# One tile for two heads' queries, keys and values, or two

## The chip, the cores and the metric

The kernel runs on one core of a Trainium2 chip. The metric is the device time of one execution in microseconds. The core's engines are TensorE (PE, matmuls; PEld is its weight load), VectorE (DVE), ScalarE (ACT), GpSimd (POOL) and SyncE (SP), whose queue issues every DMA of this kernel.

## What is computed

Attention with a band, then two MLP blocks, for 2 batches of 768 positions, 8 heads of 64 and a model width of 512. Cut to what matters:

```python
keep = is_global | is_local               # the first 8 keys, and the last 96
scores = scale * (q @ k.T) - slopes * dist
scores = where(keep, scores, -1e9)
a = exp(scores - max) ; a = a / (sum(a) + 1e-9)
x = a @ v                                 # (B, H, S, D), brought to (B, S, H*D)
# block 1: over positions, then over channels
h = maximum(x.T @ w_tok1, 0) @ w_tok2     # 768 -> 256 -> 768
u = x + h.T
u = u + maximum(u @ w_ch1, 0) @ w_ch2     # 512 -> 1536 -> 512
# block 2: a gated block with weights over positions
h = maximum(u @ w_in, 0) ; uu, vv = split(h)
out = (uu * (w_spatial @ norm(vv) + b)) @ w_out
```

## The kernel before

The attention works on 8 head pairs (2 batches x 4), called pair 0 to pair 7 here. Of each pair the host lays out one block of 128 partitions: first the queries and keys (`QK` = 1696 columns), then the values, copied into the arrangements that the bands need (2176 columns). Each pair has 3 units of 256 positions. Two units at a time form a group (`group`, line 518), 12 groups in all. For a group TensorE computes scores (`scores`, line 484), VectorE adds the bias and takes the row minimum (line 501), ScalarE does the exponentials (line 505), TensorE transposes the result (line 511), ScalarE mostly copies it to SBUF (`pt`, line 349), and TensorE multiplies with the values, in two steps (`main`, line 539, and `rest`, line 549). The context is copied (`ct`), transposed back (line 572) and scaled (line 579). "One head" below is one head of one unit: 4 heads to a group, three transposes to a head.

After two pairs of a batch their columns go through the first MLP over positions (`tok`, line 716, matmuls of lines 344 to 346 on `xh` and `xl`, the token mixing). Its weights come in 6 slices through `weight` (line 366): a DMA of 512 KB (line 389), two ScalarE passes (lines 390 and 391) and seven more steps that split each number into a high and a low part. From some 100 us on the rest of the kernel is matmuls in threes (`mm3`, lines 344 to 346) for the channel MLP and the second block.

Nothing is written in the order in which it runs. Every operation goes to a planner (`Plan`, line 98) with the engines that may do it, a cost, and the tiles that it reads and writes. The planner takes the operation that can start first, by its own costs, and among equals the one with the longest chain of work behind it. So a changed dependency changes the order of every engine. Three rules bear on the change:

- A tile is a `Buf` (line 72) with a slot and a depth. With depth 2, a new tile's first operation waits for all users of the tile two before it in the slot (`evicts`). Every other user of a tile waits for that first operation, and first operations of one slot keep their order (`prior`).
- `load_raw` (line 434) makes one tile for a pair, slot `raw`, depth 2, and loads it with two DMAs (line 445): queries and keys first, values second. Pair 0 lies in a tile of its own (`first`) and is loaded before the planner begins.
- The queue of SP is free from 7.5 on (`START`), on the planner's own clock, and the queries and keys of pair 1 may not be loaded before 8.5 (`RAW_AT`).

TensorE's idle time in the beginning is filled by the planner with 80 matmuls on zeros (line 598, `IDLE`).

Of the kernel before, what the change touches and what calls it, by code (L numbers as in the profile page):

```python
# [6 lines left out]
F32 = mybir.dt.float32  # L7
# [9 lines left out]
P = 128  # L17
B, H, S, D = 2, 8, 768, 64
# [4 lines left out]
QK = S + SEQ  # L23
# [5 lines left out]
RAW = QK + (VB - 2) * 2 * D  # L29
# [38 lines left out]
def q_at(t):  # L68
    return (t - 2) * P if t > 1 else 512 + t * P
# [141 lines left out]
def dma(nbytes):  # L211
    return ("SP", max(nbytes / 400e3, 0.5))
# [73 lines left out]
class Arm:  # L286
# [146 lines left out]

    def load_raw(self, b, hp):
        if (b, hp) == (0, 0):
            self.raws[b, hp] = lambda: self.raw0
            for key, t in zip("abv", (4.6, 6.4, 8.0)):
                self.plan.known(("raw0", key), t)
            self.plan.known(("dist",), 5.6)
            self.rawk[b, hp] = None  # L440
            return
        r = self.raws[b, hp] = self.buf("att", "raw", [P, RAW], F32, 2)
        self.rawk[b, hp] = r
        for k, sl in enumerate((slice(0, QK), slice(QK, RAW))):
            o = self.plan.op([dma(P * (sl.stop - sl.start) * 4)], lambda e, sl=sl: self.SY.dma_start(r()[:, sl], self.A["qkv"][b, hp, :, sl]),
                             [], [(r, k)])
            o.ready = RAW_AT.get((hp, k), 0.0) if b == 0 else 0.0

    def band_bias(self, b, h):
# [18 lines left out]
    def scores(self, units):  # L468


        T = self.T
        banks = [[self.bank("s", SB) for i in range(2)] for _ in units]
        for k, (b, hp, u) in enumerate(units):
            tiles = self.tiles(u)

            def make(e, k=k, b=b, hp=hp, tiles=tiles):
                raw = self.raws[b, hp]
                for t, o, w in tiles:
                    for x in range(2):
                        k0 = S + (160 * t - P + D * x if t else 0)  # L480
                        q0 = q_at(t) + D * x
                        for i in range(2):
                            r = raw()[i * D:i * D + D]
                            T.matmul(banks[k][i]()[x * D:x * D + D, o:o + w], lhsT=r[:, q0:q0 + D], rhs=r[:, k0:k0 + w],  # L484
                                     start=True, stop=True)

            self.plan.op([("PE", sum(w for _, _, w in tiles) * 0.00175)], make, [(self.rawk[b, hp], 0) if self.rawk[b, hp] else ("raw0", "ab"[u > 0])],
                         [(x,) for x in banks[k]], mode="quarters")
        return banks

# [27 lines left out]
    def group(self, units):  # L518
# [9 lines left out]
        rs = self.buf("att", "rs", [P, 2, 2, 2, 1], F32, 4)  # L528
        pts = [[self.unit(b, 2 * hp + i, u, banks[k][i], rs, k) for i in range(2)] for k, (b, hp, u) in enumerate(units)]
        cs = [self.bank(f"c{j}", CB[j]) for j in range(2)]  # L530
        val = lambda b, hp: self.raws[b, hp]()[:, QK:].rearrange("p (t h x) -> p t h x", h=2, x=D)

        def main(e):
            for k, (b, hp, u) in enumerate(units):
# [15 lines left out]
                                     rhs=pts[k][h]()[r, 2 * P + x * D:2 * P + x * D + D], start=False,  # L550
                                     stop=(x == 1 and k == max(z for z in range(2) if units[z][2] or j)))

        rk = [(self.rawk[b, hp], 1) if self.rawk[b, hp] else ("raw0", "v") for b, hp, _ in units]
        ps = [(p,) for x in pts for p in x]
        op([("PE", 0.88)], main, ps + rk, [(c,) for c in cs], mode="columns")
        op([("PE", 0.44)], rest, ps + rk, [(c,) for c in cs], mode="quarters")
# [10 lines left out]
        for j, c in enumerate(cs):  # L567
# [7 lines left out]
            for k0, k1 in ((0, 2),) if one else ((0, 1), (1, 2)):  # L575
                b, hp, u = units[k0]
# [470 lines left out]
```

## Time and profile before

| what | value |
|---|---|
| median of 3 runs (lowest to highest) | 476.6 us (476.33 to 477.08) |
| the profiled execution | 476.65 us |
| its span, first to last instruction | 474.9 us |
| mean granted TensorE clock | 0.998 |
| instructions | 8988 |

The profile shows one execution. The span is what the instructions cover; 476.65 - 474.9 = 1.75 us of the execution lie around it. Busy time of an engine is time with an instruction running on it. Matmuls overlap and their ends are modelled, so their steps are best read from start to start. "L484" is line 484 of the kernel before. A releaser is what ended an engine's idle time.

### The profile page before, as it was taken

Reading aid. Unit: us, or ns where it says so; the run is one execution under the profiler, and the core shown is the slowest. Engines: PE = TensorE matmul, PEld = TensorE weight load, DVE = VectorE, ACT = ScalarE, POOL = GpSimd, SP = SyncE. Lnnn points to the kernel's source line nnn. Section 1 sums busy time; section 2 is a strip of 40 time slices with the busy share of each in tenths; the row PEclk is TensorE's granted clock in tenths of the full one; section 3 lists DMA queues with packets and bytes.
Section 4 is the critical chain, followed back from the end, with each engine's and each line's share of the span. In section 5 each row is a group of like instructions: output and inputs, shape, how many; then the busy total and the mean of one; then the engine's idle time right before and its main releaser. Section 6 shows DMA issues by size and latency. Waiting matters only on the chain.

```text
span 474.9 us, 8988 instructions
## 1 busy us (share of the span) xinstructions
PE 469.1 (99%) x3557; PEld 414.3 (87%) x3557; DVE 291.0 (61%) x781; ACT 210.3 (44%) x531; POOL 7.8 (2%) x17
## 2 busy tenths in 40 slices
PE   9999999999999999999999999999999999999996
PEld 5887888899988888888888888888999988899985
DVE  4899999979988787113977833247942503722520
ACT  5998899974645564101435311123612122411121
POOL 0111010000000000000000000000000000000000
PEclk9999999999999999999999999999999999999999
DMA  7955749223242433000043302110000021000012
GB/s 261 391 212 209 282 159 342 78 94 127 101 169 94 160 109 132 0 1 1 3 149 115 123 33 68 33 35 0 2 0 2 0 81 53 1 0 1 0 46 95
DMA packets 12000, 44.65 MB, mean 94 GB/s; under 512 B 1456, under 2 KB 1968, under 8 KB 10928
## 3 DMA queue, kind: packets, MB, share of 16 engines
q1 hardware_dynamic: 11952, 44.01, 26.0%
q8 instruction: 30, 0.49, 0.4%
q14 instruction: 18, 0.15, 0.1%
HBM read 40.86 MB, written 3.15 MB: 93 GB/s over the span
## 4 chain that ended last, share of the span: by engine, by line
PE 98%; DMA 1%; DVE 0%; issue 0%
PE p L344 27%; PE p L345 27%; PE p L346 27%; PE p L484 4%; PE p L511 4%; PE p L539 3%; PE p L598 2%; PE p L549 1%; DMA raw<-in_qkv 1%; PE p L743 1%; PE p L572 1%; PE dummy L259 1%; DVE c L349 0%; DVE zero L251 0%; DVE shift L253 0%
## 5 line engine op out<-in xcount | busy, mean ns | idle before, releaser
L344 PE MATMUL p<-raw,w 128*128 128x512 f32 (+1 forms) x192 | 64.8, 337 | 0.0
L345 PE MATMUL p<-raw,w 128*128 128x512 f32 (+1 forms) x192 | 64.7, 337 | 0.0
L346 PE MATMUL p<-raw,w 128*128 128x512 f32 (+1 forms) x192 | 64.6, 336 | 0.0
L790 ACT ACTIVATE raw<-p 128x512 fp32r<-128x512 f32 (+1 forms) x48 | 23.6, 491 | 85.1 <-PE p L346 78.3
L791 DVE SCALAR_TENSOR_TENSOR raw<-p,raw 128x512 fp32r<-128x512 f32 (+1 forms) x48 | 26.2, 554 | 35.4 <-ACT raw L790 35.0
L505 ACT ACTIVATE e<-e,nm 128x192 f32<-128x192 f32 (+1 forms) x96 | 42.4, 455 | 4.3 <-DVE nm L501 4.3
L346 PE MATMUL p<-uy1h,w 128*128 128x512 f32 (+2 forms) x128 | 43.2, 337 | 0.0
L346 PE MATMUL p<-uy0h,w 128*128 128x512 f32 (+2 forms) x128 | 43.2, 337 | 0.0
L345 PE MATMUL p<-uy1l,w 128*128 128x512 f32 (+2 forms) x128 | 43.1, 337 | 0.0
L345 PE MATMUL p<-uy0l,w 128*128 128x512 f32 (+2 forms) x128 | 43.1, 337 | 0.0
L344 PE MATMUL p<-uy1h,w 128*128 128x512 f32 (+2 forms) x128 | 43.1, 337 | 0.0
L344 PE MATMUL p<-uy0h,w 128*128 128x512 f32 (+2 forms) x128 | 43.1, 337 | 0.0
L390 ACT ACTIVATE c<-raw 128x512 bf16<-128x512 bf16 x42 | 28.6, 680 | 28.3 <-DMA raw<-in_w_in 12.6
L346 PEld LDWEIGHTS p<-raw,w 128*128 128x128 f32 x192 | 36.1, 188 | 4.2
L344 PEld LDWEIGHTS p<-raw,w 128*128 128x128 f32 x192 | 36.1, 188 | 4.1
L345 PEld LDWEIGHTS p<-raw,w 128*128 128x128 f32 x192 | 36.1, 188 | 4.0
L501 DVE CUSTOM_DVE_ANT_0 e<-p,bias 128x192 f32<-128x192 f32 (+1 forms) x96 | 27.5, 341 | 6.2 <-PE p L484 6.1
L397 DVE SCALAR_TENSOR_TENSOR a<-raw,q 128x512 f32<-128x512 uint32 x42 | 28.8, 686 | 0.4
L355 DVE TENSOR_TENSOR a<-a,c 128x512 f32<-128x512 f32 x42 | 28.8, 686 | 0.2
L391 ACT ACTIVATE c<-raw 128x512 bf16<-128x512 bf16 x42 | 28.3, 673 | 0.0
L355 DVE TENSOR_TENSOR w<-a,w 128x512 fp32r<-128x512 f32 x36 | 24.6, 685 | 2.8 <-ACT w L349 2.7
L355 DVE TENSOR_TENSOR c<-p,bsp 128x384 f32<-128x384 f32 x16 | 8.9, 558 | 28.1 <-PE p L346 28.1
(153 smaller groups left out, 1072.6 us busy)
## 6 DMA issues: line engine op xcount, KB each, us to landing
raw<-in_wch SPq DMA_DIRECT2D x24, 512.0 KB, 3.7
raw<-in_qkv SPq DMA_DIRECT2D x7, 1088.0 KB, 8.6
raw<-in_qkv SPq DMA_DIRECT2D x7, 848.0 KB, 6.3
raw<-in_w_in SPq DMA_DIRECT2D x8, 512.0 KB, 3.8
raw<-in_wt SPq DMA_DIRECT2D x6, 512.0 KB, 7.4
out<-a SPq DMA_DIRECT2D x11, 256.0 KB, 2.0
raw<-in_w_sp SPq DMA_DIRECT2D x6, 384.0 KB, 2.9
raw<-in_w_out SPq DMA_DIRECT2D x4, 512.0 KB, 3.9
```

Source lines behind the costliest of these rows:

```text
L344: T.matmul(o, lhsT=w[0], rhs=x[0], start=first, stop=False)
L345: T.matmul(o, lhsT=w[0], rhs=x[1], start=False, stop=False)
L346: T.matmul(o, lhsT=w[1], rhs=x[0], start=False, stop=last)
L355: self.eng[e].tensor_tensor(out=o, in0=a, in1=b, op=op)
L390: op([act(n)], lambda e: self.SC.mul(pw(), top(), 2.0 ** -112), [(w,)], [(c, 0)])
L391: op([act(n)], lambda e: self.SC.activation(sg(), top(), AF.Sign), [(w,)], [(c, 1)])
L397: op([dve(n)], lambda e: V.scalar_tensor_tensor(out=aa(), in0=mid(), scalar=2.0 ** -36, in1=qq(), op0=ALU.mult, op1=ALU.mult), [(w,), (q,) ...
L484: T.matmul(banks[k][i]()[x * D:x * D + D, o:o + w], lhsT=r[:, q0:q0 + D], rhs=r[:, k0:k0 + w], start=True, stop=True)
L501: op([dve(w)], lambda e, j=j, o=o, w=w, bs=bs: V.tensor_tensor_reduce(out=e_()[:, o:o + w], in0=s()[:, o:o + w], in1=bias()[:, bs], scale= ...
L505: op([act(w, 0.2)], lambda e, j=j, o=o, w=w: SC.activation(e_()[:, o:o + w], e_()[:, o:o + w], AF.Exp, bias=nm()[:, j:j + 1], scale=-1.0, ...
L790: op([act(n)], lambda e, m=m, r=r, sl=sl, n=n: SC.activation(r()[:, 0, sl], m()[:, :n], AF.Relu), [(m,)], [(r, z, 0)])
L791: op([dve(n)], lambda e, m=m, r=r, sl=sl, n=n: V.scalar_tensor_tensor(out=r()[:, 1, sl], in0=m()[:, :n], scalar=0.0, in1=f32(r()[:, 0, sl] ...
```

## The change

Queries with keys, and values, of a pair get a tile each: slot `raw` with 1696 columns and slot `val` with 2176, both of depth 2. The scores read the first, the value products the second. Nothing else changes: the same loads, the same computation, the same planner. The changed file is one line shorter, so its lines from 443 on are one lower (L444 is the load that was L445).

```diff
     def load_raw(self, b, hp):
         if (b, hp) == (0, 0):
-            self.raws[b, hp] = lambda: self.raw0
+            self.raws[b, hp] = [lambda: self.raw0[:, :QK], lambda: self.raw0[:, QK:]]
...
-        r = self.raws[b, hp] = self.buf("att", "raw", [P, RAW], F32, 2)
-        self.rawk[b, hp] = r
+        r = self.raws[b, hp] = self.rawk[b, hp] = [self.buf("att", "raw", [P, QK], F32, 2), self.buf("att", "val", [P, RAW - QK], F32, 2)]
         for k, sl in enumerate((slice(0, QK), slice(QK, RAW))):
-            o = self.plan.op([dma(P * (sl.stop - sl.start) * 4)], lambda e, sl=sl: self.SY.dma_start(r()[:, sl], self.A["qkv"][b, hp, :, sl]),
-                             [], [(r, k)])
+            o = self.plan.op([dma(P * (sl.stop - sl.start) * 4)], lambda e, k=k, sl=sl: self.SY.dma_start(r[k](), self.A["qkv"][b, hp, :, sl]),
+                             [], [(r[k],)])
             o.ready = RAW_AT.get((hp, k), 0.0) if b == 0 else 0.0
...
-                raw = self.raws[b, hp]
+                raw = self.raws[b, hp][0]
...
-        val = lambda b, hp: self.raws[b, hp]()[:, QK:].rearrange("p (t h x) -> p t h x", h=2, x=D)
+        val = lambda b, hp: self.raws[b, hp][1]().rearrange("p (t h x) -> p t h x", h=2, x=D)
```

The keys by which scores and value products name what they read follow in the same way. Two things follow from the planner's rules: a slot of queries and keys is given back by the pair's last scores alone, and the values of a pair no longer wait for the first operation of a tile that they share with the queries.

How the change moves instructions, at three places.

SP's queue, from its first DMA behind the branch. `in_wt` is a weight slice; 128x1696 are queries and keys, 128x2176 values. Before, raw_227, raw_329, raw_619 and raw_899 (further on, behind two more slices) are pairs 1 to 4:

```order
L389 DMA raw_212<-in_wt 128x2048
L445 DMA raw_227<-in_qkv 128x1696
L445 DMA raw_227<-in_qkv 128x2176
L445 DMA raw_329<-in_qkv 128x1696
L445 DMA raw_329<-in_qkv 128x2176
L389 DMA raw_435<-in_wt 128x2048
L389 DMA raw_465<-in_wt 128x2048
L445 DMA raw_619<-in_qkv 128x1696
L445 DMA raw_619<-in_qkv 128x2176
```

And now, where val_212 with raw_255 is pair 1, raw_297 with val_393 pair 2, raw_465 with val_642 pair 3, and raw_726 pair 4:

```order
L444 DMA val_212<-in_qkv 128x2176
L444 DMA raw_255<-in_qkv 128x1696
L444 DMA raw_297<-in_qkv 128x1696
L389 DMA raw_337<-in_wt 128x2048
L389 DMA raw_360<-in_wt 128x2048
L444 DMA val_393<-in_qkv 128x2176
L444 DMA raw_465<-in_qkv 128x1696
L389 DMA raw_507<-in_wt 128x2048
L444 DMA val_642<-in_qkv 128x2176
L389 DMA raw_701<-in_wt 128x2048
L444 DMA raw_726<-in_qkv 128x1696
```

Pair 1's values stand first, ahead of its queries and keys; the first weight slice stands behind three loads of pairs 1 and 2; and the queries and keys of pairs 3 and 4 stand ahead of, or apart from, their values.

ScalarE's order from the exponentials of the fourth head. Before, with L390 and L391 the two passes over the first weight slice, and the 128-column exponential at the end pair 1's first:

```order
L505 ACTIVATE e,rs<-e,nm 128x192 x2
L390 ACTIVATE c<-raw 128x512
L349 COPY pt<-p_258 128x384
L349 COPY pt<-p_272 128x384
L505 ACTIVATE e,rs<-e,nm 128x192 x4
L391 ACTIVATE c<-raw 128x512
L505 ACTIVATE e,rs<-e,nm 128x128
L505 ACTIVATE e,rs<-e,nm 128x192
```

And now:

```order
L504 ACTIVATE e,rs<-e,nm 128x192 x3
L349 COPY pt<-p_258 128x384
L349 COPY pt<-p_269 128x384
L504 ACTIVATE e,rs<-e,nm 128x192 x3
L349 COPY ct<-p_301 128x256
L349 COPY ct<-p_304 128x256
L349 COPY pt<-p_331 128x384
L349 COPY pt<-p_339 128x384
L504 ACTIVATE e,rs<-e,nm 128x128
L504 ACTIVATE e,rs<-e,nm 128x192 x2
L504 ACTIVATE e,rs<-e,nm 128x128
L390 ACTIVATE c<-raw 128x512
```

The two passes over the first weight slice moved behind pair 1's first four exponentials, and four copies moved ahead of these.

TensorE's order where the token mixing begins (L344 to L346 on xh and xl). Before:

```order
L598 LDWEIGHTS zero
L598 MATMUL p_154<-zero 128x256
L344 MATMUL p_949<-xh,wth 128x256
L345 MATMUL p_949<-xl,wth 128x256
L346 MATMUL p_949<-xh,wtl 128x256
L598 LDWEIGHTS zero
L598 MATMUL p_154<-zero 128x256
L344 MATMUL p_959<-xh,wth 128x256
L345 MATMUL p_959<-xl,wth 128x256
L346 MATMUL p_959<-xh,wtl 128x256
L539 MATMUL p_963<-pt,raw 64x64 x4
```

And now:

```order
L483 MATMUL p_1052<-raw 64x192
L483 MATMUL p_1054<-raw 64x192
L510 MATMUL p_1066<-ident,e 128x128 x3
L344 MATMUL p_1076<-xh,wth 128x256
L345 MATMUL p_1076<-xl,wth 128x256
L346 MATMUL p_1076<-xh,wtl 128x256
L344 MATMUL p_1083<-xh,wth 128x256
L345 MATMUL p_1083<-xl,wth 128x256
L346 MATMUL p_1083<-xh,wtl 128x256
L510 MATMUL p_1088<-ident,e 128x128 x3
```

The last of the 80 zero matmuls stood between the first token matmuls; now all 80 stand ahead of pair 4's first scores. The token mixing begins behind the transposes of 26 heads (three sets of pair 4's scores done), where it began behind those of 24 (none of pair 4's done).

## Rows read from the trace of the kernel before

**Rows 1.** The page, busy time of the engines over the whole span.

```profile
PE 469.1 (99%) x3557; PEld 414.3 (87%) x3557; DVE 291.0 (61%) x781; ACT 210.3 (44%) x531; POOL 7.8 (2%) x17
```

**Rows 2.** Stretches: us, then busy us (x count) by engine, clock, DMA share, GB/s.

```profile
10.00:20.00 10.00, 9.95 (x154) 8.01 (x156) 7.23 (x38) 9.27 (x36) 0.88 (x2) 1.00 1.02 419
20.00:30.00 10.00, 10.00 (x208) 7.92 (x201) 9.23 (x44) 9.96 (x39) 1.23 (x2) 1.00 0.41 145
30.00:40.00 10.00, 10.00 (x163) 8.03 (x163) 9.99 (x45) 9.92 (x39) 1.46 (x2) 1.00 0.60 237
40.00:50.00 10.00, 9.32 (x171) 8.03 (x170) 7.89 (x33) 7.34 (x25) 1.43 (x2) 1.00 0.84 292
...
300.00:400.00 100.00, 100.00 (x524) 90.62 (x523) 44.79 (x85) 26.84 (x50) 0.00 (x0) 1.00 0.07 24
```

**Rows 3.** The chain of waits in order of time: start us, us, what.

```profile
12.34 1.00 PE p L598 x9
13.34 1.27 PE p L539 x28
14.64 0.89 PE p L484 x14
...
20.80 1.07 PE p L539 x28
...
41.13 6.31 DMA raw<-in_qkv
...
49.99 0.81 PE p L484 x16
50.80 0.80 PE p L511 x6
```

**Rows 4.** TensorE's time line: start us, us, engine, line, count, [idle before, releaser].

```profile
47.49 0.78 PE L484 MATMUL p<-raw 64*64 64x128 f32 x16 [0.62 <-DMA raw<-in_qkv]
...
49.12 0.28 PE L344 MATMUL p<-xh,wth 128*128 128x256 f32 x1
...
49.47 0.28 PE L344 MATMUL p<-xh,wth 128*128 128x256 f32 x1
```

**Rows 5.** ScalarE's time line, the same columns.

```profile
12.45 0.67 ACT L390 ACTIVATE c<-raw 128x512 bf16<-128x512 bf16 x1 [0.73 <-DMA raw<-in_wt]
...
14.20 0.45 ACT L505 ACTIVATE e<-e,nm 128x192 f32<-128x192 f32 x1
...
14.64 0.46 ACT L505 ACTIVATE e<-e,nm 128x192 f32<-128x192 f32 x1
...
16.08 0.40 ACT L505 ACTIVATE e<-e,nm 128x128 f32<-128x128 f32 x1
...
18.73 0.38 ACT L349 COPY ct<-p 128x256 f32<-128x256 f32 x1
18.98 0.50 ACT L349 COPY pt<-p 128x384 f32<-128x384 f32 x1
19.35 0.49 ACT L505 ACTIVATE e<-e,nm 128x192 f32<-128x192 f32 x1
...
24.14 0.68 ACT L390 ACTIVATE c<-raw 128x512 bf16<-128x512 bf16 x1
24.72 0.66 ACT L391 ACTIVATE c<-raw 128x512 bf16<-128x512 bf16 x1
...
42.57 0.21 ACT L505 ACTIVATION_READ_ACCUMULATOR e<-e,nm 128x1 f32 x1
...
48.78 0.40 ACT L505 ACTIVATE e<-e,nm 128x128 f32<-128x128 f32 x1 [2.66 <-DVE nm L501]
```

**Rows 6.** DMA issues: out<-in, queue, count, KB each, median us to landing.

```profile
raw<-in_qkv SPq DMA_DIRECT2D x7, 1088.0 KB, 8.6
raw<-in_qkv SPq DMA_DIRECT2D x7, 848.0 KB, 6.3
...
raw<-in_wt SPq DMA_DIRECT2D x6, 512.0 KB, 7.4
```

More of the change, by code (lines that the diff above doesn't have):

```diff
@@ L485, in make @@
                                      start=True, stop=True)
-            self.plan.op([("PE", sum(w for _, _, w in tiles) * 0.00175)], make, [(self.rawk[b, hp], 0) if self.rawk[b, hp] else ("raw0", "ab"[u > 0])],
+            self.plan.op([("PE", sum(w for _, _, w in tiles) * 0.00175)], make, [(self.rawk[b, hp][0],) if self.rawk[b, hp] else ("raw0", "ab"[u > 0])],
                          [(x,) for x in banks[k]], mode="quarters")
@@ L551, in rest @@
                                      stop=(x == 1 and k == max(z for z in range(2) if units[z][2] or j)))
-        rk = [(self.rawk[b, hp], 1) if self.rawk[b, hp] else ("raw0", "v") for b, hp, _ in units]
+        rk = [(self.rawk[b, hp][1],) if self.rawk[b, hp] else ("raw0", "v") for b, hp, _ in units]
         ps = [(p,) for x in pts for p in x]
```

## Prediction, made before the changed kernel had run

> **What bounds the kernel now.** I read the page first: TensorE is busy 99% of the span [rows 1]. That figure counts overlapping matmuls, so it can hide short waits, and the stretches come next [rows 2]. From 300 to 400 us TensorE is busy without a break while ScalarE is busy for 27 of 100 us: there TensorE alone sets the pace, and nothing that the change touches lies there. Between 10 and 50 us it is different: VectorE and ScalarE are nearly full (9.99 and 9.92 of 10 us from 30 to 40), and in the stretch from 40 to 50 all three fall (PE 9.32, DVE 7.89, ACT 7.34). Third, the chain of waits says why [rows 3]: at 41.13 it leaves the engines and runs for 6.31 us through the transfer of a head pair's queries, keys and values. The rows of TensorE's time line show the end of it: the scores at 47.49 come after 0.62 us of idling, put down to that transfer [rows 4]. So the stage up to some 50 us is limited by ScalarE and VectorE, with TensorE in step; from where the token mixing fills TensorE, its own queue decides, and a microsecond lost before that on TensorE is a microsecond at the end.
>
> One more thing has to be seen before any sum. 80 matmuls on zeros (line 598) stand in TensorE's order to fill its idle time; nine take 1.00 us [rows 3], so all 80 cost 80 x 0.111 = 8.9 us. The change keeps 80. They are spent whether or not there is idle time to fill, so the work in TensorE's queue is the same before and after, and **the time can only move by what TensorE waits**. The waits that rows show up to 50 us are small: 0.62 us at 47.49 [rows 4], 0.2 us before 14.64 (the 28 products at 13.34 last 1.27 us; the same 28 at 20.80 last 1.07) [rows 3]; together 0.8 us.
>
> **The change part by part, against the profiled execution (476.65 us; the median of the three runs is 476.6).**
>
> *Queries and keys of pair 4 are free to come earlier.* Before, their slot is that of pair 2 with its values, given back after pair 2's last value product: issue at 41.13, needed at 47.49. Now the slot needs only pair 2's last scores, some ten microseconds of work earlier in the order. The wait at 47.49 should go: -0.6 us on TensorE, and ScalarE's 2.66 us of idling before 48.78 [rows 5] with it.
>
> *Pair 1's queries and keys come later.* In the queue's order the values of pair 1 now stand first, where a weight slice stood. That puts 1088 instead of 512 KB ahead of them [rows 6]. The transfers run at their limit then (419 GB/s from 10 to 20 us, share 1.02 [rows 2]), so the scores of pair 1 move from 14.64 by 576 x 1024 / 419e3 = 1.4 us, to 16.05. The Trainium skill's "DMA: Bandwidth & Descriptors", section "Queues, rings and completion order", says that a DMA engine takes descriptors in ring order, though completions may overtake each other; by the second half the queries might not lose all 1.4 us. No row of before shows one overtaking. TensorE itself hardly waits for it: the new order puts two more zero matmuls (0.22), the products (1.07), their rest and six transposes ahead of these scores, which takes it from 13.34 to about 15.9. That is 0.15 us of waiting for the 0.2 us of before.
>
> *ScalarE pays.* Pair 1's first exponential came 1.44 us after the start of its scores (16.08 against 14.64 [rows 3, 5]); now it comes at 17.5. Ahead of it stand four exponentials and two copies that no longer have a weight slice between them: from about 12.0 they need 4 x 0.44 + 2 x 0.37 us and end at 14.5, then come four copies (2 x 0.25 + 2 x 0.37 = 1.24 us) until 17.5. Of 3.0 us, 1.8 are idle; with 0.3 before 12.0 that is 2.1 us, against the 0.73 before 12.45 [rows 5]: **1.4 us more**. The first weight slice, converted from 12.45 on before, now follows 1088 + 848 + 848 KB of head pairs and lands near 19.2 by the same rate. Nothing hides ScalarE's loss at once, since it is 99% busy until 41 us; it is paid back only by the 2.66 us at 48.78.
>
> *Where the two meet.* The token mixing (line 344 on xh, xl) starts after 24 heads' transposes before and after 26 in the new order, and by then all 80 zero matmuls are gone. So I count ScalarE's queue to the 26th head. Before, the 24th head's exponentials end at 42.57 + 0.21 = 42.8 [rows 5]. The new queue adds up to the 26th: two heads, 2 x (2 x 0.44 + 0.37) = 2.5; one and a half weight slices, 1.5 x 2 x 0.58 = 1.74; two context copies, 0.5; a copy of 768 columns, 0.74 (estimate: twice the 0.37 of 384 columns). That is 5.5, and with the 1.4 us of idling the 26th is ready at 49.7. A hand-over (0.2: from the end of the scores at 47.49 + 0.78 to the exponential at 48.78 lie 0.5 us with a reduction in between [rows 4, 5]) and its transposes (0.4, half of the six at 50.80 [rows 3]) bring TensorE to 50.3. Nothing in this sum waits for TensorE, so 50.3 is a floor. The ceiling adds one late slice (1.16) and the 1.4 us once more: 52.9. I take 50.8, near the floor, since ScalarE's rows from 20 to 40 us hold only 0.1 us of idling and the new order has the same alternation of work [rows 2].
>
> *Is that early or late?* Before, the 26th head's transposes end at 50.80 + 0.80 = 51.6 [rows 3]. TensorE had then done 15 token matmuls (five threes of 0.35 [rows 4], 1.76 us) that the new order still has ahead, and the new order has done one more set of scores (0.81 [rows 3]). The difference of work is 0.95 us, so it breaks even at 51.6 - 0.95 = 50.65. At 50.8 the change is worth +0.15 us, at the floor -0.35, at the ceiling +2.25. Later in the order TensorE has token mixing to do between the heads in both, the loads come with more room, and I cost it at nothing. What hides that is the backlog of token matmuls; without it each further late head would cost what it is late.
>
> The sum: 476.65 + 0.15 = **476.8 us**, no change that can be measured. Within 0.2% means within 0.95 us of 476.6, about what a measurement of this kernel can tell from no change: 475.65 to 477.55.
>
> **The rivals.**
>
> *Faster: more was hidden than the rows show.* Weight loads on TensorE are busy 8.03 of 10 us from 30 to 40 but 90.62 of 100 from 300 to 400 [rows 2]. If that were all waiting, there would be 1.0 us in each 10, 4 us from 10 to 50, and earlier loads could free some of it. Against it: the releasers name a load only at 47.49 and at 14.64, and small score and value matmuls load smaller weights. A third of it, 1.3 us, gives 475.35. The Trainium skill's "Perfetto Trace Analysis", section "Identifying the Most-Contended Engine", holds just this view: matmul busy time is no measure of TensorE's room, LDWEIGHTS busy share is. The traces bear out that the shares differ, not that a load is the cause. Chance 0.17.
>
> *Slower: pair 1's late scores set the pace.* One place, ScalarE's queue from 14.5 to 20 us: if its 1.4 us of extra idling, and the first weight slice's lateness, are not paid back by the removed 2.66 us before TensorE has run out of zero matmuls, then TensorE waits for transposes of the heads just before the token mixing. It decides once the 26th head's transposes end later than 51.6 (break-even plus 0.95). At the ceiling of 52.9 that is 476.65 + 2.25 = 478.9. For it: ScalarE and VectorE are nearly full from 20 to 41 us, so a loss there has no slack to vanish in [rows 2]. Against it: 2.66 us of slack at 48.78 go. Chance 0.33.
>
> *It doesn't do what it says.* The load of pair 4's queries stands in SP's queue behind a weight slice, which waits for a slot of its own to be converted. If that slice is late, pair 4 still waits: the 0.6 us stay, while pair 1's loss is there: 476.65 + 0.15 + 0.6 = 477.4, within the bound. Chance 0.04.
>
> **How the numbers follow.** Forecast 0.46, faster 0.17, slower 0.33, no effect 0.04. The range reaches from the faster rival's price to the slower one's: 475.4 to 478.9, with about one in ten left out on either side. Faster by over 0.2%: 0.17. Within 0.2%: 0.46 + 0.04 = 0.50. Slower by over 0.2%: 0.33.
>
> **What the profile after would show.** Right: no idling of TensorE for a load of queries near 47 us and none of ScalarE's 2.66 us; the load of pair 4's queries issued near 30 us; pair 1's scores at about 16.0 and its first exponential at 17.5, with ScalarE idle about 2 us before; the first weight slice converted near 19 us; the first token matmul near 51 us; TensorE without gaps from there. Wrong: scores of pair 1 still near 14.6 (then overtaking happens), the first token matmul after 52 us (slower), or gaps of TensorE between 55 and 105 us, for which I have no term.

## The result, and the profile after

| | median | lowest to highest | runs |
|---|---|---|---|
| before | 476.84 us | 476.33 to 477.08 | 4 |
| after | 480.01 us | 479.61 to 480.85 | 4 |

The ratio is 1.0054 with a 95% interval of 1.0035 to 1.0073: the change makes the kernel **slower by 0.5%**. By the ratio that is 2.6 us; the two medians lie 3.2 us apart, which is still inside the interval. The median of after lies above the range that was predicted (475.4 to 478.9). The profiled execution of after took 480.08 us, with a span of 478.0 us; before it was 476.65 and 474.9. The spans differ by 3.1 us.

The page of after, against [rows 1]:

```profile
PE 469.6 (98%) x3557; PEld 413.6 (87%) x3557; DVE 291.3 (61%) x779; ACT 210.9 (44%) x533; POOL 7.1 (1%) x17
```

TensorE has the same number of instructions and 0.5 us more busy time. So some 2.6 of the 3.1 us are time in which it does nothing. The stretches of after show where (busy us of PE, PEld, DVE, ACT, POOL with counts, then clock, DMA share, GB/s), against [rows 2]:

```profile
10.00:20.00 10.00, 8.87 (x140) 6.98 (x140) 4.06 (x24) 7.12 (x28) 0.88 (x2) 1.00 1.01 420
20.00:30.00 10.00, 9.65 (x180) 7.42 (x182) 9.15 (x49) 10.00 (x35) 0.92 (x2) 1.00 0.58 213
30.00:40.00 10.00, 10.00 (x179) 8.00 (x172) 9.86 (x39) 10.00 (x39) 1.30 (x2) 1.00 0.69 252
40.00:50.00 10.00, 9.64 (x193) 7.30 (x191) 9.88 (x47) 10.00 (x34) 1.03 (x2) 1.00 0.84 280
...
60.00:70.00 10.00, 9.64 (x125) 8.01 (x126) 9.38 (x41) 10.00 (x32) 0.46 (x1) 1.00 0.31 97
70.00:80.00 10.00, 9.16 (x140) 8.07 (x139) 9.58 (x37) 10.00 (x34) 0.50 (x1) 1.00 0.71 266
...
300.00:400.00 100.00, 100.00 (x530) 90.84 (x529) 44.35 (x84) 26.44 (x49) 0.00 (x0) 1.00 0.06 22
```

The kernel before in the two later stretches:

```profile
60.00:70.00 10.00, 10.00 (x131) 8.86 (x122) 10.00 (x36) 10.00 (x36) 1.22 (x2) 1.00 0.35 121
70.00:80.00 10.00, 10.00 (x152) 9.02 (x151) 9.96 (x39) 9.70 (x31) 0.00 (x0) 1.00 0.95 361
```

Read the first figure after the comma. From 10 to 30 us TensorE loses 1.08 + 0.35 us against before; from 40 to 50 it wins 0.32 (the wait for pair 4 is gone); from 60 to 80 it loses 0.36 + 0.84. Also look at VectorE and ScalarE from 10 to 20: 4.06 and 7.12 us, where before they were busy for 7.23 and 9.27. From 300 to 400 us nothing differs.

Part of the last two differences is only a matter of where the window is cut: after's scores of pair 0 start at 10.02 us in its trace, before's at 10.55. Counted from 0 to 20 us (before first), VectorE is busy for 2.7 us less in after, ScalarE for 1.6 us less:

```profile
0.00:20.00 20.00, 18.84 (x219) 12.75 (x223) 11.82 (x66) 13.85 (x49) 1.54 (x7) 1.00 0.88 327
```

```profile
0.00:20.00 20.00, 17.44 (x210) 11.91 (x211) 9.15 (x56) 12.23 (x44) 1.55 (x7) 1.00 0.88 328
```

TensorE's time line of after at the places where the two kernels part:

```profile
16.65 0.77 PE L483 MATMUL p<-raw 64*64 64x128 f32 x16 [1.13 <-DMA raw<-in_qkv]
...
51.14 0.36 PE L344 MATMUL p<-xh,wth 128*128 128x256 f32 x1
...
66.36 1.24 PE L538 MATMUL p<-pt,val 128*64 128x64 f32 x20 [0.21 <-DVE first L578]
...
75.73 0.92 PE L538 MATMUL p<-pt,val 128*64 128x64 f32 x24 [0.65 <-DVE first L578]
```

The first is the wait for pair 1's queries; the chain of waits of after gives their landing, 5.34 + 11.18 = 16.5 us:

```profile
5.34 11.18 DMA raw<-in_qkv
16.65 0.77 PE p L483 x16
```

ScalarE's time line of after shows pair 1's first exponential and the first pass over a weight slice, against [rows 5]:

```profile
17.83 0.40 ACT L504 ACTIVATE e<-e,nm 128x128 f32<-128x128 f32 x1 [1.69 <-DVE nm L500]
...
19.90 0.68 ACT L390 ACTIVATE c<-raw 128x512 bf16<-128x512 bf16 x1 [0.32 <-DMA raw<-in_wt]
```

VectorE meets pair 1's scores with a wait of 4.74 us in after:

```profile
17.49 0.29 DVE L500 CUSTOM_DVE_ANT_0 e<-p,bias 128x128 f32<-128x128 f32 x1 [4.74 <-PE p L483]
```

and of 1.87 us in the kernel before:

```profile
15.57 0.29 DVE L501 CUSTOM_DVE_ANT_0 e<-p,bias 128x128 f32<-128x128 f32 x1 [1.87 <-PE p L484]
```

### The profile page after: what moved, and what is told of

Read it like the earlier page. It is cut to its first block, busy times and chain, and to the rows that moved or that the text cites. A ratio compares the mean times of both kernels' runs of the same rounds, so it can differ in the third digit from the quotient of the medians.

```text
span 478.0 us, 8986 instructions
## 1 busy us (share of the span) xinstructions
PE 469.6 (98%) x3557; PEld 413.6 (87%) x3557; DVE 291.3 (61%) x779; ACT 210.9 (44%) x533; POOL 7.1 (1%) x17
## 4 chain that ended last, share of the span: by engine, by line
PE 89%; DMA 4%; ACT 4%; DVE 1%; issue 1%; SPq 0%; ACTq 0%; DVEq 0%
PE p L344 27%; PE p L346 26%; PE p L345 26%; PE p L510 2%; DMA raw<-in_qkv 2%; PE p L483 2%; ACT e L504 2%; PE p L538 2%; DMA raw<-in_wch 2%; PE p L571 1%; PE p L597 1%; PE p L742 1%; PE p L548 1%; ACT pt L349 1%; DMA nt<-in_n 1%
## 5 line engine op out<-in xcount | busy, mean ns | idle before, releaser
L344 PE MATMUL p<-raw,w 128*128 128x512 f32 (+1 forms) x192 | 64.8, 338 | 0.0
L346 PE MATMUL p<-raw,w 128*128 128x512 f32 (+1 forms) x192 | 64.6, 336 | 0.0
L390 ACT ACTIVATE c<-raw 128x512 bf16<-128x512 bf16 x42 | 28.6, 682 | 38.5 <-DMA raw<-in_w_in 14.6
L504 ACT ACTIVATE e<-e,nm 128x192 f32<-128x192 f32 (+1 forms) x96 | 42.6, 463 | 2.6 <-DVE nm L500 2.5
L346 PE MATMUL p<-uy1h,w 128*128 128x512 f32 (+2 forms) x128 | 43.2, 337 | 0.0
L346 PE MATMUL p<-uy0h,w 128*128 128x512 f32 (+2 forms) x128 | 43.1, 337 | 0.0
L344 PE MATMUL p<-uy0h,w 128*128 128x512 f32 (+2 forms) x128 | 43.1, 337 | 0.0
L344 PE MATMUL p<-uy1h,w 128*128 128x512 f32 (+2 forms) x128 | 43.1, 337 | 0.0
L346 PEld LDWEIGHTS p<-raw,w 128*128 128x128 f32 x192 | 36.1, 188 | 4.2
L344 PEld LDWEIGHTS p<-raw,w 128*128 128x128 f32 x192 | 36.1, 188 | 4.1
L391 ACT ACTIVATE c<-raw 128x512 bf16<-128x512 bf16 x42 | 28.5, 678 | 0.0
L345 PEld LDWEIGHTS p<-uy1l,w 128*128 128x128 f32 x128 | 24.1, 188 | 2.3
```

Of the source, the lines that this page charges most:

```text
L344: T.matmul(o, lhsT=w[0], rhs=x[0], start=first, stop=False)
L345: T.matmul(o, lhsT=w[0], rhs=x[1], start=False, stop=False)
L346: T.matmul(o, lhsT=w[1], rhs=x[0], start=False, stop=last)
L390: op([act(n)], lambda e: self.SC.mul(pw(), top(), 2.0 ** -112), [(w,)], [(c, 0)])
L391: op([act(n)], lambda e: self.SC.activation(sg(), top(), AF.Sign), [(w,)], [(c, 1)])
L504: op([act(w, 0.2)], lambda e, j=j, o=o, w=w: SC.activation(e_()[:, o:o + w], e_()[:, o:o + w], AF.Exp, bias=nm()[:, j:j + 1], scale=-1.0, ...
```

## Experiments

All were timed against the kernel before on the chip that ran them; its median was 477.2 to 477.7 us there, so kernels are compared by their ratios. Two theories stood at the start. **A**: with pair 1's values first, VectorE and ScalarE run dry before 20 us, and TensorE pays from 60 to 76 us. **B**: a channel slice (`in_wch`) lands late, at 59 us, because the queue is fuller there.

### Is it the split, or the order that puts pair 1's values first?

*Queries first in the queue alone.* The orders of all engines are kept; SP only issues pair 1's queries ahead of its values.

```diff
+            def load(e, k=k, sl=sl):
+                go = lambda: self.SY.dma_start(r[k](), self.A["qkv"][b, hp, :, sl])
+                if (b, hp, k) == (0, 1, 1):
+                    self.held = go
+                    return
+                go()
+                if (b, hp, k) == (0, 1, 0):
+                    self.held()
...
```

> The changed kernel with every engine's order kept, but SP issues the queries and keys of pair 1 ahead of the values of pair 1 (the changed kernel: behind them). Theory A (the values that stand first cost the 3.2 us: VectorE idles 4.74 us and TensorE 1.13 us for pair 1's scores, and the debt is paid between 60 and 76 us): these queries land about 2.6 us sooner (1088 KB less ahead of them at 419 GB/s), TensorE's 1.13 us are gone, VectorE's idling falls to about 3.5 us, and the time falls by 1.1 to 1.5 us, to 478.5 to 478.9. Theory B (the early loss is made up by 50 us, and the loss comes from the channel weight slice that lands late at 59 us): TensorE starts its token mixing sooner but waits longer between 60 and 76 us, the time stays within 0.4 us of 480.0.

Measured: 480.76 us, ratio 1.0070 (1.0051 to 1.0090). TensorE no longer waits for pair 1's queries, and nothing is won. It waits for ScalarE's copies instead (us in total, times, longest; L517 is after's L510):

```profile
PE p L517 <- ACT pt L349: 2.1, 4, 0.9
```

where after has

```profile
PE p L510 <- ACT pt L349: 0.9, 3, 0.4
```

*Queries before values, planned anew.* Each load of values depends on the load of its own pair's queries; the slots stay split.

```diff
-                             [], [(r[k],)])
+                             [(r[0],)] if k else [], [(r[k],)])
```

> The changed kernel with one dependency more for the planner: a pair's values are loaded only after its queries and keys. Slots stay apart; every order is planned anew, and SP begins as before the change (weight slice, queries of pair 1), with queries of pair 2 ahead of values of pair 1. Theory A: the loss goes with its cause; pair 1's scores near 14.6, no idling of VectorE over 2 us there, and 476 to 477.2 us, as before the change or a little better for the loads that come sooner. Theory B (split slots crowd the queue at 43 to 52 us, whatever the start): the late channel slice and TensorE's waits between 60 and 76 us stay, and the time is 478.5 us or more.

Measured: 477.83 us, ratio 1.0007 (0.9992 to 1.0022): the kernel before's time. The split slots cost nothing by themselves. In this kernel ScalarE waits 1.37 us for a channel slice at 56.85, and the time is none the worse, so such a wait alone is no loss.

*Only pair 1's values later, planned anew.*

```diff
-RAW_AT = {(1, 0): 8.5}
+RAW_AT = {(1, 0): 8.5, (1, 1): 8.6}
```

> The changed kernel, with one entry added to the table of earliest times: pair 1's values may not start before 8.6 (its queries keep 8.5), so the planner puts the first weight slice and pair 1's queries ahead of them, as in the kernel before; everything else stays free, and the order is planned anew. Theory C (the loss belongs to the order that the planner makes when pair 1's values stand first, not to the slots): the kernel before's time within 0.3%, about 477. Theory D (the slots, of which the later loads of other pairs make use, cost the time): about 480, as the changed kernel.

*Values of pair 1 first, but one tile as before.*

```diff
-        for k, sl in enumerate((slice(0, QK), slice(QK, RAW))):
+        parts = list(enumerate((slice(0, QK), slice(QK, RAW))))
+        for k, sl in parts[::-1] if (b, hp) == (0, 1) else parts:
```

> The kernel before, one tile for queries, keys and values, only that pair 1's values are loaded ahead of its queries; planned anew. Its queue then begins as the changed kernel's does: values 1, queries 1, queries 2. Theory C: slower by 2 to 4 us (479 to 481) without any split. Theory D: no change by more than 0.3%, about 477.

Measured: split with pair 1's values later, 478.11 us, ratio 1.0018 (1.0001 to 1.0035); one tile with the values first, 480.80 us, ratio 1.0084 (1.0063 to 1.0104). The pair settles the question: with pair 1's values first the loss is there without any split, and with the split it is nearly gone once they stand behind the queries. VectorE's row for pair 1's scores in the first of the two:

```profile
15.85 0.29 DVE L500 CUSTOM_DVE_ANT_0 e<-p,bias 128x128 f32<-128x128 f32 x1 [2.01 <-PE p L483]
```

and in the second:

```profile
17.12 0.29 DVE L502 CUSTOM_DVE_ANT_0 e<-p,bias 128x128 f32<-128x128 f32 x1 [3.55 <-PE p L485]
```

The first is like before (1.87), the second nearer to after (4.74). Where the loss is paid is not the same: in the second TensorE idles for 1.32 + 1.01 us from 50 to 70, in after for 1.2 from 60 to 80.

### Data that land late, or orders that put work late?

*The first four transfers as in the kernel before* (weight slice, pair 1's queries, its values, pair 2's queries), orders of TensorE, VectorE and ScalarE kept. The three loads of pairs 1 and 2 are held until the first weight slice has been issued.

```diff
+            for go in self.held:
+                go()
...
+                if (b, hp) in ((0, 1), (0, 2)) and (hp == 1 or k == 0):
+                    self.held.insert(0 if (hp, k) == (1, 0) else len(self.held), go)
```

> The changed kernel with the orders of TensorE, VectorE and ScalarE kept word for word, and the first four transfers in the order of the kernel before (weight slice, pair 1's queries, its values, pair 2's queries). If the loss comes by data that land late (slice at 19.9, queries at 16.5), it goes: about 477. If it lies in the engines' orders, which put that work later whenever the data land, it stays: 479.5 to 481. I expect the second, since queries first alone gave nothing.

Measured: 479.81 us, ratio 1.0050 (1.0031 to 1.0069). The four transfers in their old order do not help where the engines' orders put the work late.

*The channel slice ahead of pair 5's values* (theory B), orders kept; the same kind of edit, for pair 5.

> The changed kernel with every engine's order kept, but SP issues the channel weight slice that landed at 59 us ahead of the values of pair 5 (1088 KB). Theory B: it lands 2 us or more sooner, ScalarE's 0.82 us of idling before 59.15 goes, and the time falls by 0.8 us or more, to 479.2 or less. Theory A: ScalarE's 0.82 us go as well, but VectorE's debt is what TensorE waits for at 66 and 75 us, and the time falls by less than 0.4 us.

Measured: 480.16 us, ratio 1.0063 (1.0043 to 1.0082). ScalarE's 0.82 us wait at 59.15 is gone, but ScalarE waits 1.2 us for a later channel slice instead, and TensorE 1.16 us for a copy at 80.12. Theory B in this form falls.

*Less work for VectorE* (theory A): the 12 additions to the row sums.

```diff
-        op([("DVE", 0.08)], lambda e: V.tensor_scalar(out=rs(), in0=rs(), scalar1=1e-9, scalar2=None, op0=ALU.add), [], rks)
+        op([("DVE", 0.08)], lambda e: None, [], rks)
```

> The changed kernel with every order kept, leaving out the addition of 1e-9 to the row sums: 12 small VectorE instructions, 2.5 us of VectorE in all, 9 of them behind 20 us. Theory A in the form that VectorE is the engine in debt: from 20 to 76 us it has no slack, so the 7 instructions up to there give back 0.07 to 0.2 us each, and TensorE's waits for VectorE's scaling near 66 and 75 us shrink: 479.0 to 479.4 us. If ScalarE is the engine in debt, or late transfers are (theory B), VectorE's time is free and the time stays within 0.3 us of 480.0.

Measured: 480.85 us, ratio 1.0074 (1.0058 to 1.0090). So these additions are not the cause, though the rows of after named VectorE. Whether VectorE's lateness plays a part is not shown by it.

### Are the zero matmuls spent in any case?

Every second one of the 80 is left out, in the kernel before, in after, and in the split kernel with queries first.

```diff
-            o = plan.op([mm(256, 1)], lambda e: self.T.matmul(
+            o = plan.op([mm(256, 1)], lambda e, i=i: i % 2 == 0 and self.T.matmul(
```

> The kernel before with every second one of the 80 zero matmuls left out; the engines' orders are otherwise kept. The prediction took them as spent in any case: then 40 x 0.111 = 4.4 us go, 472.5. The rival: they stand where TensorE would wait for ScalarE and VectorE anyway, and what is left out turns into waiting: 477 within 0.3%. In between, the share that is saved is the share of the zero matmuls that is no filler. If the clock falls for lack of them, slower than 478.

> The split slots with every pair's queries ahead of its values (planned anew, which timed 1.0007 of the kernel before), and every second zero matmul left out. In the kernel before, leaving them out only lengthened the wait for pair 4's queries (1.7 us instead of 0.6). That wait is gone here. If zero matmuls are a cost on TensorE's path: faster than the kernel before by 1 us or more, 474 to 476.5. If they only fill what ScalarE and VectorE leave open: the same, 477 to 478.5.

> The changed kernel, orders kept, with every second zero matmul left out. If the extra 3 us are zero matmuls that no longer find idle time to fill, 4.4 us less in TensorE's queue take back 2 to 3 us: 477 to 478. If TensorE waits for the other engines there, nothing: 479.5 to 481.

Measured, each with 40 of the 80: before 478.17 us (ratio 1.0022, 1.0002 to 1.0041), split with queries first 477.75 (1.0009, 0.9994 to 1.0024), after 479.95 (1.0044, 1.0027 to 1.0061). None is faster than its kernel with all 80 by more than the interval; leaving out 40 x 0.111 = 4.4 us of TensorE's work is worth nothing. TensorE's waits by the line that waited, in the kernel before with 40 of them:

```profile
PE p L484 <- DMA raw<-in_qkv: 1.7, 1, 1.7
PE dummy L259 <- DVE epst L254: 1.0, 1, 1.0
PE p L511 <- ACT pt L349: 0.5, 2, 0.3
```

The wait for pair 4's queries, 0.62 us in [rows 4], is 1.7 us here, and from 10 to 50 us TensorE idles for 2.60 us instead of 0.73. The zero matmuls stood in waits and hid them.

### Which part of the order?

In the next kernels single operations of the changed kernel's planned sequence are moved, by their place in it; everything else is emitted in the same order. `32: [90, 55]` takes operations 90 and 55 from their places and puts them behind operation 32. The line numbers of these kernels are 13 higher (L517 is L504). The first kernel also has the first four transfers as before.

```diff
-            o.fn(e)
+            seq.append((o, e))
...
+            put = {32: [90, 55], 86: [94], 106: [113, 101, 104, 105], 128: [137, 125, 126]}
```

> The changed kernel with its planned sequence edited by hand in one stretch: the first four transfers stand as in the kernel before (weight slice, pair 1's queries, its values, pair 2's queries), and on TensorE the first three sets of scores after pair 0's are moved ahead: the first to between the products and their rest, the second and third to before the seven zero matmuls that stood ahead of each. VectorE's and ScalarE's orders are untouched. Theory E (VectorE and ScalarE run dry from 15 to 20 us because these scores stand late in TensorE's queue, and what they lose there is the 3 us): most of it comes back, 477 to 478. Rival F (what costs is later: the order after 40 us, with ScalarE and VectorE blocked behind weight slices): 479.5 to 481, as with the transfers alone.

*And the first weight slice early on ScalarE* (`88: [119, 123]` added):

> The same, and on ScalarE the two passes of the first weight slice stand where the kernel before had room for them: ahead of the context copies at about 14.5, instead of after the exponentials at 19.9. Theory E: 477 or a little under, at least as fast as the run without it. Rival F: 479.5 to 481. A third outcome, faster than the kernel before by 0.3% or more, would say that the split has a worth of its own which the order hides.

Measured: 480.38 us, ratio 1.0057 (1.0039 to 1.0075), and 478.81 us, ratio 1.0028 (1.0015 to 1.0040). ScalarE's time line of the first tells why early scores gave nothing:

```profile
16.38 0.65 ACT L362 COPY ct<-p 128x256 f32<-128x256 f32 x2 [1.28 <-PE p L561]
...
17.71 0.41 ACT L517 ACTIVATE e<-e,nm 128x128 f32<-128x128 f32 x1
```

and of the second:

```profile
14.89 0.66 ACT L403 ACTIVATE c<-raw 128x512 bf16<-128x512 bf16 x1
15.45 0.67 ACT L404 ACTIVATE c<-raw 128x512 bf16<-128x512 bf16 x1
16.28 0.65 ACT L362 COPY ct<-p 128x256 f32<-128x256 f32 x2 [0.16 <-PE p L561]
...
17.61 0.41 ACT L517 ACTIVATE e<-e,nm 128x128 f32<-128x128 f32 x1
```

The context copies stand ahead of pair 1's exponentials in ScalarE's queue. They wait for value products that the scores have pushed back, so the exponentials start at 17.71, hardly earlier than in after (17.83). With the slice's two passes in that hole, 1.2 us of ScalarE's work is done in time that it idled, and the median falls by 1.6 us (the intervals of the two ratios just touch).

*The slice alone*, with the transfers and without the scores (`put = {32: [90, 55], 88: [119, 123]}`):

> The changed kernel with the first four transfers as in the kernel before, and on ScalarE the first weight slice ahead of the context copies; no scores, no scaling moved. Theory G's first part (ScalarE's queue: 1.3 us of conversion done in time that it otherwise idles): 478.5 to 479, as with the scores moved too. If the early scores are needed as well: 479.5 to 481.

Measured: 479.19 us, ratio 1.0040 (1.0026 to 1.0054), between the transfers alone (1.0050) and scores with slice (1.0028), and told apart from neither.

*The late waits.* Two scalings move ahead of the reductions that stand before them on VectorE (`485: [491], 551: [556]`), in the better kernel and in after itself:

> The run with early scores and an early slice (1.0028 of the kernel before), and on VectorE two scalings moved ahead of the two reductions that stood before each: those at about 64.5 and 74, for which TensorE's value products waited 0.20 and 0.64 us there. The second part of theory G (what is left of the loss is TensorE waiting from 60 to 76 us for scalings that stand late in VectorE's order): 0.6 to 0.9 us faster than that run, 477.8 to 478.2 and its ratio 1.001 to 1.0015. Rival H (these waits are only the visible end of VectorE's and ScalarE's lateness and come back elsewhere): no change, 478.8.

> The changed kernel with only the two scalings on VectorE moved ahead of the reductions before them. Theory G's second part: 0.6 to 0.9 us faster than the changed kernel, 479.0 to 479.6, ratio about 1.004. Rival H: no change, 480 to 480.8.

Measured: 479.06 us (ratio 1.0032, 1.0018 to 1.0045) and 480.99 us (1.0075, 1.0058 to 1.0092): no gain. TensorE's time line ahead of the move, in the kernel with early scores and slice:

```profile
74.38 0.92 PE L551 MATMUL p<-pt,val 128*64 128x64 f32 x24 [0.64 <-DVE first L591]
```

with the scalings moved in it:

```profile
73.88 1.32 PE L551 MATMUL p<-pt,val 128*64 128x64 f32 x32 [0.30 <-DVE first L591]
...
80.57 0.55 PE L523 MATMUL p<-ident,e 128*128 128x128 f32 x3 [1.34 <-ACT pt L362]
```

and moved in after:

```profile
74.74 1.32 PE L551 MATMUL p<-pt,val 128*64 128x64 f32 x32 [0.31 <-DVE first L591]
...
81.20 0.55 PE L523 MATMUL p<-ident,e 128*128 128x128 f32 x3 [1.11 <-ACT pt L362]
```

The wait at 74 us halves, and a new one of over 1 us stands at 81. ScalarE's time line of the kernel with both names what is behind it:

```profile
77.77 0.67 ACT L403 ACTIVATE c<-raw 128x512 bf16<-128x512 bf16 x1 [1.08 <-DMA raw<-in_wch]
```

ScalarE got there before the channel slice had landed, and the copy that TensorE needs stood behind the slice's pass.

*Pair 1's exponentials ahead of the context copies*, as in the kernel before, on top of all this (`106: [113, 102, 108, 93, 89, 115, 95, 117, 92, 96, 99, ...]`):

> The same, and on ScalarE pair 1's first exponentials stand ahead of the context copies, as in the kernel before (with the context transposes and scalings that hang on them moved behind the second scores). Theory G: VectorE and ScalarE then lose nothing more than in the kernel before between 14 and 20 us, and the time is the kernel before's or under, 476.5 to 477.8. Rival H: 478 to 479, no better than the run beside it.

Measured: 480.78 us, ratio 1.0075 (1.0057 to 1.0092), slower than the kernel that it was built on. ScalarE's time line shows a wait that the kernel it was built on doesn't have:

```profile
53.05 0.66 ACT L403 ACTIVATE c<-raw 128x512 bf16<-128x512 bf16 x1 [1.67 <-DMA raw<-in_wt]
```

The early piece, in an otherwise unchanged order, ran into the next fixed thing, here a weight slice.

*Two loads of values behind the channel slices*, with the scalings, and with the slice alone (`401: [380], 547: [526]`):

> The run with early scores, early slice and early scalings (1.0032), in which ScalarE stood 0.91 us at 58 and 1.08 us at 78 for a channel slice and TensorE 1.34 us at 80.6 behind it. Here the two loads of values that stood in SP's queue ahead of those two slices are moved behind them. Theory J (what the engines gain early is given back at these slices, because the slices queue behind head pairs' loads): the waits of ScalarE at 58 and 78 shrink below 0.4 us each and the time falls by about 1 us, to 478.0. If the slices are late for another reason (their staging slot is freed late by VectorE), or the loss comes back elsewhere: no change, 479.

> The run with the early slice alone (1.0040, ScalarE's waits for a channel slice 0.54 at 57 and 0.23 at 83), with the same two loads of values moved behind the slices. Theory J: at most 0.5 us faster, 478.7 to 479.2. Otherwise no change.

Measured: 478.88 us (ratio 1.0035, 1.0018 to 1.0052) and 478.42 us (1.0021, 1.0010 to 1.0032). The stretches of the kernel with the scalings, before these loads were moved:

```profile
70.00:80.00 10.00, 8.74 (x136) 7.82 (x136) 9.86 (x37) 8.92 (x29) 0.00 (x0) 1.00 0.82 292
80.00:90.00 10.00, 9.43 (x135) 8.61 (x136) 8.32 (x33) 9.99 (x34) 0.00 (x0) 1.00 0.44 147
```

and with them moved:

```profile
70.00:80.00 10.00, 9.57 (x146) 8.64 (x145) 9.67 (x39) 10.00 (x33) 0.00 (x0) 1.00 0.78 268
80.00:90.00 10.00, 9.76 (x135) 8.66 (x134) 9.44 (x33) 8.99 (x30) 0.00 (x0) 1.00 0.37 131
```

ScalarE's waits at 58 and 78 us are gone, TensorE is busier by 0.83 + 0.33 us in these twenty, and ScalarE has a new hole of 1.0 us from 80 to 90. The median does not move by more than its interval: theory J isn't borne out there. The other of the two, the slice alone with the loads behind, is the best with pair 1's values placed first by the planner. Its interval and that of after don't overlap, so these edits together (first four transfers, slice, two loads) do win back some 1.6 of the 2.6 us (by the ratios 1.0054 and 1.0021); which of them how much is not settled.

## Why the prediction was wrong

**Right.** *Pair 4's queries come earlier*: issued at 31.83 us, where "near 30" was said; no wait at 47 us and no 2.66 us of ScalarE's idling. *Pair 1's queries come later*, and no overtaking: the values issued ahead of them at 4.96 landed 9.5 us later, at 14.5, they at 16.5. The Trainium skill's "DMA: Bandwidth & Descriptors", section "Queues, rings and completion order", says that descriptors are taken in ring order, while a later one may finish first; in this trace these loads landed in the order of issue. *ScalarE pays*: first exponential at 17.83 for 17.5, first slice at 19.90 for 19.2; and by 20 us it had been busy for 1.6 us less than in before, in three kernels with after's order of ScalarE up to there for 1.3 to 1.4 less (12.46, 12.51 and 12.58 us in the table below), where the term said 1.4. *Where the two meet*: first token matmul at 51.14 for 50.8. And the slower rival named one place where work was lost, ScalarE's queue from 14.5 to 20 us.

**Not what costs: pair 1's wait.** The scores came at 16.65 instead of 16.05, and TensorE waited 1.13 us in one piece instead of 0.15. But that wait differs between executions of one order. Four kernels of the experiments have after's orders of work up to there. In the one with half the zero matmuls it is 1.17 us, in the one with the scalings early 0.99; in the one without the additions and in the one with the channel slice ahead of pair 5's values TensorE comes to these scores without a listed wait,

```profile
16.18 0.77 PE L483 MATMUL p<-raw 64*64 64x128 f32 x16
```

```profile
16.49 0.78 PE L494 MATMUL p<-raw 64*64 64x128 f32 x16
```

and the ratios of these two are 1.0074 and 1.0063. What had no term at all is VectorE, with 2.7 us less by 20 us; whether that costs is not shown.

**Mis-sized: the break-even.** At 51.14 the prediction's own line gives 51.14 - 50.65 = +0.5 us. Its difference of work, 0.95 us, left out that the kernel before had also done two context transposes more by then (22 against 20; four take 0.44 us); with them the line gives +0.7. ScalarE, too, had three copies more to do up to the 26th head than its sum had. The stretches of TensorE give 1.08 + 0.35 - 0.32 = 1.1 us between 10 and 50. So at the first token matmul the loss was some 0.7 to 1.1 us, against the 0.15 of the forecast.

**Failed: "Later in the order ... I cost it at nothing".** This is the step that carries most of the error: some 2 of the 3.1 us between the spans came after the first token matmul. From 60 to 80 us the stretches show 1.2 us of TensorE's idling; the rest isn't listed as idling. The cover that was named, the backlog of token matmuls, did not hide it, and the prediction had said itself that gaps from 55 us on would prove it wrong. The kernel with the channel slice ahead of pair 5's values shows it most plainly:

```profile
10.00:50.00 40.00, 39.48 (x692) 30.79 (x694) 34.53 (x160) 38.51 (x139) 4.12 (x8) 1.00 0.78 286
50.00:100.00 50.00, 47.90 (x675) 42.86 (x668) 47.44 (x175) 48.82 (x161) 2.27 (x4) 1.00 0.55 190
```

From 10 to 50 us its TensorE idles for 0.52 us, less than the 0.73 of before; from 50 to 100 for 2.10, where before shows none; and its ratio is 1.0063. ScalarE is busy for 10.00 of 10 us from 60 to 80 in after, and nearly so in before (10.00 and 9.70). That it carries the early debt up to there is a reading, not shown.

**Failed: "the time can only move by what TensorE waits", as a way to forecast.** As bookkeeping it nearly holds: up to 100 us TensorE idles for 2.7 us more in after (0.3 of them before 10 us), and 0.5 us more busy time makes up the difference of the spans. But it took the 80 zero matmuls as spent in any case, and the runs with 40 of them show the opposite: they hide waits that the trace doesn't list, and the waits that it does list are not prices. Removing a listed wait gave nothing four times (pair 1's queries, the channel slice at 59 us, the scalings twice): it came back as another one. The Trainium skill's "Perfetto Trace Analysis", section "Optimization Strategy", advises to find the gaps of the engine in question and what blocks it, and to make that start sooner. In this kernel the rows at 75.73 led to VectorE's scalings in just that way, and starting them sooner was worth nothing (1.0075 against 1.0054).

**The other rivals.** The faster one fell: nothing hidden came free, and weight loads are busy for 8.00 of 10 us from 30 to 40 as they were before (8.03 in [rows 2]). That the change doesn't do what it says fell too, with pair 4's load at 31.83.

**What is shown, and what stays open.** Shown: the loss belongs to the order that is planned when pair 1's values stand first in SP's queue. It is there without the split (1.0084), and gone or nearly gone with it once they stand behind the queries (1.0007, 1.0018). It is not the landing of the first transfers by itself (1.0070, 1.0050), and not the split slots. How that order costs the time is in part open. Three readings of every kernel's profile in us, sorted by ratio (half the zero matmuls leave more idle time up to 50 us by themselves):

| kernel | ScalarE busy, 0 to 20 | TensorE idle, 10 to 50 | TensorE idle, 50 to 100 | ratio |
|---|---|---|---|---|
| before | 13.85 | 0.73 | 0.00 | 1 |
| split, queries first, planned anew | 14.23 | 0.29 | 0.87 | 1.0007 |
| the same, half the zero matmuls | 13.28 | 3.11 | 0.55 | 1.0009 |
| split, pair 1's values later | 13.57 | 0.41 | 0.37 | 1.0018 |
| slice early, loads behind | 13.84 | 0.36 | 1.00 | 1.0021 |
| before, half the zero matmuls | 14.87 | 2.60 | 0.00 | 1.0022 |
| scores and slice early | 13.51 | 0.37 | 1.19 | 1.0028 |
| the same, scalings early | 13.41 | 1.31 | 2.24 | 1.0032 |
| the same, loads behind | 14.02 | 0.36 | 1.11 | 1.0035 |
| slice early | 13.89 | 0.39 | 1.10 | 1.0040 |
| after, half the zero matmuls | 12.78 | 3.26 | 1.93 | 1.0044 |
| first four transfers as before | 13.09 | 0.34 | 2.71 | 1.0050 |
| after | 12.23 | 1.84 | 1.25 | 1.0054 |
| scores early | 12.55 | 0.43 | 1.27 | 1.0057 |
| channel slice ahead of pair 5's values | 12.58 | 0.52 | 2.10 | 1.0063 |
| queries first in the queue alone | 12.13 | 1.06 | 2.70 | 1.0070 |
| without the additions | 12.51 | 0.89 | 2.81 | 1.0074 |
| pair 1's exponentials first | 13.13 | 1.42 | 3.37 | 1.0075 |
| after, scalings early | 12.46 | 1.72 | 2.11 | 1.0075 |
| one tile, pair 1's values first | 12.44 | 0.59 | 2.36 | 1.0084 |

Down the table ScalarE's busy time before 20 us falls and TensorE's idle time from 50 us on grows, while its idle time up to 50 us follows neither. These are single profiles, and it is a tendency, not a law: slice early has as much of ScalarE's work done by 20 us as before, and 1.0040. Open is how the rest of the loss, about 0.4 of it by 1.0021 and 1.0054, divides over the order after 40 us. A third staging buffer for the slices, which might take the waits for them away, wasn't tried. No version was found that is faster than the kernel before.

## What to carry to other kernels

Where a planner sets the order, ask first what the change puts at the head of the queue, and undo that alone by one added dependency or start time; that told more here than any reading of waits. Filler work on an engine hides its waits, so count it out before calling that engine the bound. And a wait in the trace is a place where engines meet, not a price: take it away in a run before you add it to a sum, and see whether a second execution of the same order has it.

## What was not expected of the hardware

Leaving out 40 of the 80 zero matmuls did not lower the granted clock: its mean was 0.999, 1.000 and 0.998 in the three kernels, and 0.998 and 1.000 in before and after with all 80, so the upper of its two levels (2.4 GHz) nearly throughout. The busy time of TensorE in the first 10 us varies between executions by more than some of the terms argued over (8.89 us in before, 8.58 in after, 8.03 in the kernel with one tile and the values first, whose scores of pair 0 waited 0.65 us for their load), so one profile can't carry a term of 0.3 us. And some traces hold one wait more far behind everything that was changed: TensorE waits 1.14 us for VectorE (its row for `raw<-p,raw`) at 186.99 us in the kernel that is split with queries first, and 0.97 at 256.20 in the one with the first four transfers as before; before and after have no such wait.
